# An RWKV-5 layer fused with a squared-ReLU FFN: the logarithm of w taken on a spread tile, two chunks' small matmuls interleaved, and another order in the opening

## The chip, the cores and the metric

The kernel runs on one core of one Trainium2 chip. The metric is the device time of one execution in microseconds (us), given as the median of the runs. Times inside the execution come from one profiled execution and are counted from the start of its span. The engines are named as in the profile: PE (TensorE; PEld is its weight load), DVE (VectorE), ACT (ScalarE), POOL (GpSimd) and SP (SyncE, which here only issues DMAs). Each engine works through its own instructions strictly in order and waits on semaphores for what the others produce.

## The reference

```
def _attn_ref(r, k, v, w, u):                      # (4, 8, 768, 48): batch, heads, sequence, head_dim
    state = zeros((B, H, D, D))
    for t in range(S):
        cur = einsum('bhd,bhe->bhde', u[None] * kt, vt)
        y[:, :, t] = einsum('bhd,bhde->bhe', rt, state + cur)
        state = w[None, :, :, None] * state + einsum('bhd,bhe->bhde', kt, vt)

def _moe_ref(x, w_in, w_out):                      # 3072 tokens, 384 -> 2048 -> 384
    h = maximum(x @ w_in, 0.0)
    return h * h @ w_out
```

A linear-attention recurrence with a decay `w` per head and channel is computed over 768 steps, its output is laid out as 3,072 rows of 384, and a dense layer pair with a squared ReLU between follows.

## The kernel before

The sequence is cut into chunks of 128 steps. A unit is one batch element and one chunk (24 units, list `UNITS`); within a chunk the recurrence is done in the parallel form, and a state `S0W` per batch element is handed from chunk to chunk. The decay enters as powers of w: `Wt` = exp(t·ln w) multiplies r (step `rh`), `Wk` = exp(-(t+1)·ln w) multiplies k (step `kh`). These factors come from ln w, which is laid out over all 128 partitions.

Each step of the program is a small function of class `Do`; the string `ORDER` lists all steps as `name.unit:engine/buffer` in the order in which they are put into the engines' queues. So the order on one engine is the order of that engine's entries in the string, and the place between entries of different engines has no force. The number behind the slash picks the buffer or the PSUM bank (eight banks).

The steps that matter here, for a unit i or a pair q of units:

- `w`, `u`: DMA of the two parameter rows, issued by ACT; `tab` loads ACT's table. `lw` (L266) takes Ln of the row w on one partition into `lrow`; `bw` (L269) spreads that over 128 partitions with a matmul by a row of ones into a PSUM bank; `Wt`, `Wk` (L298, L294) take Exp of that bank, scaled by a column of t. `bu`, `ub` (L272) spread u; `bc`, `WLcol`, `WLm` (L303, L309, L314) make the decay over a whole chunk.
- `lp.x.q` (L325): load of r, k or v for both units of a pair (384 KB in runs of 384 bytes), `ld.x.i` (L321): the same for a single unit (192 KB in runs of 192 bytes). SP issues both. `V.q` (L331) loads a quarter of the first FFN matrix into `W1[q]`, `W.q` (L334) a quarter of the second into `W2[q]`; GpSimd issues these, because the DMA casts to bf16 on its way.
- The first four units are done in two pairs (`PAIRED = 4`): pair 0 is both chunks 0 and 1 of batch 0, pair 1 those of batch 1. A pair's tile holds the even and the odd steps of 256 steps as two tiles of 128 partitions; partitions 0 to 63 belong to the first chunk, 64 to 127 to the second. `TR`, `TK` (L364) transpose r and k on PE, `RC`, `KC` copy the result out of PSUM (ACT, L251), `Ap` (L384) makes the scores, `Bp` (L392, DVE) masks them.
- `U.i` (L463) makes a chunk's contribution to the state, `S0` (L478) decays it into `S0W`. `Y.i` makes the output of a chunk: for a paired unit two matmuls with an identity that add `dv` (L428), four that add the old state (L436, second chunk only), and sixteen scores times v (L440).
- `P0`, `P1`, `du`, `dv` (L343, L347, L350, L355) make the bonus term with u; `vb` (L251 or L253) casts v to bf16.
- `xs` copies the output, `X` (L489) transposes it on PE, `xTc` copies that; then the FFN: `F1` (L505), `re` (relu), `sq` (square), `F2` (L533), `os`, `out`.
- `mP.0`, `mP.1`, `mJ` build the masks on GpSimd (L283, L220, L278). `Z.n` (L565) is n identity matmuls into a bank that nobody reads.

The memsets ahead of the string (L204 to L234) all run on DVE: the padding of `lrow`, the ones, the padding of the seven `rk` tiles, and `WLm`.

Of the kernel before, what the change touches and what calls it, by code (L numbers as in the profile page):

```python
# [19 lines left out]
EARLY_U = ()  # L20
COLS = (slice(0, 288), slice(288, 384))
GROUPS = [1, 1, 2, 2, 2, 2, 2, 2, 2, 2, 2, 2, 1, 1]
POOLS = dict(ldr=8, ldk=8, ldv=8, ws=3, rk=7, P=5, dv=5, vb=8, rkT=7, bank=8, Bm=8, xs=5, xT1=2, xT2=3, hr=6, hq=28,
    os=8, ts=2)
ORDER = """
w:A mP.0:G mP.1:G lp.r.0:S/0 lp.k.0:S/0 tab:A lw:A Z.8:P/0 bw:P/0 lp.r.1:S/1 lp.v.0:S/0 mJ:G u:A lp.k.1:S/1 Wt.1:A/1
lp.v.1:S/1 bc:P/2 P0.1:G/0 Wk.0:A/3 rh.1:D/0 ld.r.5:S/4 Wt.0:A/4 bu:P/5 kh.0:D/1 V.3:G WLcol:A P0.0:D/1 Wk.1:A/6
rh.0:D/1 TR.0:P/7 ld.k.4:S/4 V.0:G rh.3:D/2 ub:A V.1:G rh.2:D/3 vb.0:A/0 vb.1:A/1 ld.r.4:S/5 kh.1:D/0 P1.0:G RC.0:A/0
TR.1:P/2 kh.2:D/3 kh.3:D/2 TK.0:P/1 KC.0:A/1 V.2:G P1.1:D U.1:P/5 Z.2:P/4 TK.1:P/4 ld.k.5:S/5 du.0:D/0 dv.0:G RC.1:A/2
du.1:D/1 dv.1:G Ap.0.1:P/7/3 Bp.0.1.1:D/0 vb.3:A/2 U.0:P/6 Ap.0.0:P/1/2 Bp.0.1.0:D/1 Bp.0.0.1:D/2 WLm:G KC.1:A/3  # L30
Z.7:P/3 Ap.1.0:P/3/7 vb.2:A/3 U.3:P/2 Bp.0.0.0:D/3 P0.2:G/2 U.2:P/4 S0.0:D Y.0:P/1 ld.v.4:S/4 S0.2:D P1.2:G Y.1:P/6
xs.0:A/0 ts.3:D/0 ts.1:D/1 X.0:P/4 Ap.1.1:P/1/2 xTc.0:D/0 du.2:D/2 xs.1:A/1 X.1:P/5 F1.0.3:P/4 xTc.1:A/1 P0.3:G/3
P1.3:G Bp.1.0.1:D/4 F1.0.0:P/6 re.0.3:D/0 dv.2:G F1.1.3:P/5 Wt.2:A re.0.0:A/1 W.1:G Bp.1.1.1:D/5 du.3:D/3 ld.v.5:S/5
Bp.1.0.0:D/6 Wk.2:A F1.1.0:P/4 F1.1.1:P/6 dv.3:G re.1.0:A/2 F1.0.1:P/0 rh.5:G/4 re.1.3:A/3 Bp.1.1.0:D/7 Y.3:P/4
sq.1.3:A/0 re.0.1:A/4 W.2:G kh.4:D/5 re.1.1:A/5 sq.1.0:D/1 Y.2:P/5 ld.k.6:S/6 xs.3:D/2 W.3:G F1.0.2:P/0 xs.2:A/3
rh.4:D/5 sq.0.0:A/2 X.3:P/6 W.0:G X.2:P/4 re.0.2:D/3 F1.1.2:P/5 xTc.3:A/0 sq.0.3:A/3 xTc.2:D/0 re.1.2:A/2 P0.4:D/4
T.4:P/0 Tc.4:D/4 F1.2.4:P/6 F1.2.7:P/4 sq.1.2:D/4 F1.2.5:P/5 re.2.4:D/1 re.2.7:A/0 ld.r.6:S/6 sq.0.2:A/5 F1.2.1:P/0
re.2.5:D/2 re.2.1:A/3 sq.2.5:D/6 sq.0.1:D/7 F1.2.0:P/6 kh.5:D/4 F1.2.2:P/4 sq.2.1:A/8 F1.2.6:P/5 re.2.2:A/2 re.2.0:D/4
T.5:P/0 re.2.6:D/3 F2.0.2:P/4 F1.2.3:P/6 ld.r.7:S/7 Tc.5:A/5 P1.4:D du.4:D/4 sq.1.1:D/9 A.4:P/5/0 sq.2.6:A/10
re.2.3:A/5 sq.2.3:A/11 F2.0.1:P/4 sq.2.0:A/12 F2.0.3:P/4 vb.4:G/4 Bm.4.1:D/0 Bm.4.0:D/1 sq.2.7:A/13 P0.5:D/1 A.5:P/6/0  # L40
Bm.5.1:D/2 sq.2.4:A/14 F2.1.1:P/5 Bm.5.0:D/3 F2.1.2:P/5 ld.k.7:S/7 dv.4:G Y.4:P/0 P1.5:G du.5:D/0 F2.3.2:P/6
sq.2.2:A/15 ld.v.7:S/6 ld.k.9:S/0 xs.4:D/4 F2.0.0:P/4 vb.5:A/5 Y.5:P/0 dv.5:D xs.5:D/0 F2.3.0:P/6 P0.6:G/0 P1.6:G
ld.v.6:S/7 F2.3.1:P/6 os.0:D/0 ld.r.9:S/0 X.4:P/0 xTc.4:D/1 U.4:P/4 F2.1.0:P/5 X.5:P/0 F2.1.3:P/5 S0.4:D xTc.5:D/1
rh.7:G/6 F1.3.0:P/4 os.1:D/1 F1.3.4:P/0 P0.7:G/2 re.3.0:D/3 out.1:S F1.3.2:P/5 kh.7:D/6 re.3.4:A/5 kh.6:G/0 F1.3.6:P/4
re.3.6:A/4 ld.r.8:S/1 vb.6:A/6 re.3.2:A/0 XB.7:S/6 rh.6:D/0 F1.3.3:P/0 F2.3.3:P/6 kh.9:D/1 re.3.3:A/1 P1.7:D XB.6:S/1
F2.2.2:P/4 os.3:D/2 F1.3.1:P/5 du.7:D/1 S.1:D ld.k.8:S/1 U.5:P/0 S0.5:D dv.7:G U.6:P/6 re.3.1:A/2 sq.3.1:A/16
F2.2.3:P/4 ld.r.11:S/2 ts.6:D/1 F2.2.1:P/4 sq.3.3:D/17 P0.9:G/3 sq.3.0:A/18 ld.r.10:S/3 F2.2.0:P/4 sq.3.6:A/19
F1.3.7:P/0 os.2:D/3 du.6:D/2 A.7:P/5/6 ld.k.11:S/2 re.3.7:A/2 vb.7:G/7 F1.3.5:P/4 Bm.7.1:D/0 sq.3.2:A/20 rh.8:G/2
# [76 lines left out]
def kernel(  # L125
# [511 lines left out]
```

## Time and profile before

| | |
|---|---|
| median of 3 runs | 170.58 us (170.56 to 170.84) |
| the profiled execution's own time | 171.19 us |
| its span | 169.5 us |
| granted TensorE clock over the span | 1.00 |
| DMA, mean over the span | 163 GB/s |

How to read what follows: a row of the timeline gives the start in us from the span's start, the time from the first start to the last end of the instructions merged into it, engine, line of the kernel, operation, tile written, tiles read, shape, the count after an x, and in brackets the engine's idle time before it with what ended that. An end of a matmul is modelled, so the start of the next one is the better mark of when PE was free. The bracket of a DMA queue's row ("q1", "q0") gives packets, megabytes and the time that the packets took as a share of 16 DMA engines over the window; two packets can be in flight on one engine, so a share can exceed 100%. Queue q1 is SP's, q0 is GpSimd's.

### The profile page before, as it was taken

To read this page: it belongs to the slowest core of one execution; us is meant where nothing else is said; L and a number is where in the kernel's file an instruction comes from. 1 tells how busy PE (TensorE), PEld (TensorE's weight loads), DVE (VectorE), ACT (ScalarE), POOL (GpSimd) and SP (SyncE) were. 2 spreads that over 40 slices of the span, in tenths; PEclk is the share of its full clock that TensorE was granted. 3 is DMA by queue.
4 is the path that set the end of the run, shared out by engine and by line. 5 is a ranking of instruction groups with operands and counts; after the bars stand their busy time and mean duration, and the time that the engine had idled before them with its cause. 6 is when DMAs were issued, how large, how long until landed. Compare 5 with 4: busy or idle time off the path is not lost.

```text
span 169.5 us, 4602 instructions
## 1 busy us (share of the span) xinstructions
PE 164.2 (97%) x1828; PEld 125.4 (74%) x1828; DVE 137.1 (81%) x255; ACT 101.9 (60%) x190; POOL 99.9 (59%) x122
## 2 busy tenths in 40 slices
PE   4999999999999999999999999999999999999993
PEld 1686989767866786888766888766888676898762
DVE  5669989997899999979999999998779975955300
ACT  4684686870685779249892359952099393254731
POOL 6799681277199608996699979399627550200000
PEclk9999999999999999999999999999999999999999
DMA  5999999991899798999997999965959672230032
GB/s 136 323 237 193 215 215 208 201 200 39 165 200 211 138 191 173 209 201 134 209 203 151 212 228 220 177 136 141 184 98 202 170 88 70 90 99 0 6 139 93
DMA packets 96137, 27.56 MB, mean 163 GB/s; under 512 B 90642, under 2 KB 96020, under 8 KB 96116
## 3 DMA queue, kind: packets, MB, share of 16 engines
q1 hardware_dynamic: 92416, 22.55, 66.4%
q0 software_dynamic: 2816, 3.54, 11.5%
q10 hardware_dynamic: 884, 1.18, 2.2%
q8 instruction: 14, 0.23, 0.6%
q14 instruction: 7, 0.06, 0.1%
HBM read 20.45 MB, written 4.72 MB: 149 GB/s over the span
## 4 chain that ended last, share of the span: by engine, by line
PE 95%; ACT 1%; DVE 1%; issue 1%; ACTq 0%
PE bank L505 37%; PE bank L533 36%; PE bank L411 3%; PE bank L463 2%; PE bank L452 2%; PE bank L364 2%; PE bank L489 2%; PE bank L450 2%; PE bank L547 2%; PE bank L440 1%; PE bank L269 1%; DVE Bm L392 1%; PE bank L303 1%; PE bank L272 1%; PE bank L398 1%; PE bank L428 1%
## 5 line engine op out<-in xcount | busy, mean ns | idle before, releaser
L505 PE MATMUL bank<-xT,W 128*128 128x256 bf16 (+1 forms) x672 | 70.0, 257 | 0.0
L533 PE MATMUL bank<-W,hq 128*128 128x384 bf16 x368 | 68.9, 326 | 0.0
L505 PEld LDWEIGHTS <-W 128*128 128x128 bf16 x672 | 56.9, 98 | 7.7
L515 ACT ACTIVATE hr<-bank 128x512 bf16<-128x512 f32 x67 | 38.7, 594 | 36.4 <-PE bank L505 27.8
L533 PEld LDWEIGHTS <-hq 128*128 128x128 bf16 x368 | 33.8, 98 | 18.2
L522 ACT ACTIVATE hq<-hr 128x512 bf16<-128x512 bf16 x70 | 41.0, 626 | 3.4 <-DVE hr L517 2.8
L419 DVE TENSOR_TENSOR Bm<-bank,maskJT 128x512 bf16<-128x512 f32 x40 | 25.7, 682 | 2.7 <-PE bank L411 2.7
L355 POOL TENSOR_TENSOR dv<-ldv,du 128x384 f32<-128x384 f32 (+1 forms) x18 | 15.9, 891 | 16.2 <-DVE du L350 11.3
L517 DVE TENSOR_SCALAR hr<-bank 128x512 bf16<-128x512 f32 x29 | 19.7, 686 | 6.6 <-PE bank L505 4.5
L347 POOL TENSOR_TENSOR P<-P,ub 128x384 f32<-128x384 f32 x15 | 16.0, 1070 | 13.1 <-DVE P L343 12.7
L340 POOL TENSOR_TENSOR rk<-ldr,Wt 128x384 bf16<-128x384 f32 x15 | 16.4, 1101 | 0.0
L343 POOL TENSOR_TENSOR P<-ldr,ldk 128x384 f32<-128x384 f32 x13 | 13.3, 1023 | 1.5 <-DMA ldk<-in_k_dram 1.2
L524 DVE TENSOR_TENSOR hq<-hr 128x512 bf16<-128x512 bf16 x26 | 12.4, 490 | 2.0 <-ACT hr L515 1.8
L484 POOL TENSOR_TENSOR S0W<-ts,WLm 128x384 bf16<-128x384 f32 x10 | 10.9, 1091 | 4.4 <-DVE ts L481 3.6
L475 DVE TENSOR_TENSOR xs<-bank,dv 128x384 bf16<-128x384 f32 x20 | 11.1, 553 | 3.0 <-PE bank L452 1.1
L337 POOL TENSOR_TENSOR rk<-ldk,Wk 128x384 bf16<-128x384 f32 x12 | 12.3, 1032 | 1.4 <-DMA ldk<-in_k_dram 1.4
L350 DVE TENSOR_REDUCE du<-P 128x8 f32<-128x384 f32 x24 | 12.9, 542 | 0.0
L253 DVE COPY os<-bank 128x384 f32<-128x384 f32 x11 | 6.1, 551 | 6.9 <-PE bank L533 6.9
L481 DVE TENSOR_TENSOR ts<-bank,S0W 128x384 f32<-128x384 f32 x16 | 8.7, 550 | 1.2 <-POOL S0W L484 0.8
L452 PE MATMUL bank<-vb,Bm 128*128 128x48 bf16 x160 | 9.5, 183 | 0.0
L251 ACT COPY os<-bank 128x384 f32<-128x384 f32 (+2 forms) x14 | 6.3, 458 | 4.5 <-PE bank L533 2.5
L452 PEld LDWEIGHTS <-Bm 128*128 128x128 bf16 x160 | 8.2, 96 | 1.0
(79 smaller groups left out, 177.8 us busy)
## 6 DMA issues: line engine op xcount, KB each, us to landing
ldr<-in_r_dram SPq DMA_DIRECT2D x20, 192.0 KB, 4.0
ldk<-in_k_dram SPq DMA_DIRECT2D x20, 192.0 KB, 4.2
ldv<-in_v_dram SPq DMA_DIRECT2D x20, 192.0 KB, 3.6
out_dram<-os SPq DMA_DIRECT2D x12, 192.0 KB, 2.1
W<-in_moe_w_in_dram POOLq DMA_DIRECT2D x4, 384.0 KB, 8.6
W<-in_moe_w_out_dram POOLq DMA_DIRECT2D x4, 384.0 KB, 6.4
out_dram<-os ACTq DMA_DIRECT2D x5, 192.0 KB, 3.5
ldr<-in_r_dram SPq DMA_DIRECT2D x2, 384.0 KB, 4.1
```

What stands on the lines that cost most here:

```text
L340: e.tensor_mul(rk[slot[f"rk{i}"]][:, 0, :, 0:D], loaded("r", i), Do.factor("t", i % 2 if i < PAIRED else 2))
L343: e.tensor_mul(P0b[slot[f"P{i}"]], loaded("r", i), loaded("k", i))
L347: e.tensor_mul(t, t, bank("bu")[:, 0 : H * D].rearrange("p (h d) -> p h d", h=H) if i in EARLY_U else ub)
L350: e.tensor_reduce(dub[slot[f"dv{i}"]], P0b[slot[f"P{i}"]], axis=mybir.AxisListType.X, op=ALU.add)
L355: e.tensor_mul(dv_of(i) if i < PAIRED else dvb[slot[f"dv{i}"]], loaded("v", i), t)
L419: e.tensor_mul(Bmb[slot[f"Bm{i}{h}"]], heads(bank(f"bA{i}{h}"), 128), mask_b)
L452: e.matmul(y[:, hc, D * h : D * (h + 1)], m[h][:, hc, :], vb[:, 2 * hc + h, :], start=(c == 0), stop=True, skip_group_check=True,)
L505: e.matmul(hp[:, fi, :], W1[f // 4][:, c, 256 * (f // 2 % 2) : 256 * (f // 2 % 2 + 1)].rearrange("p (m j) -> p j m", j=2)[:, f % 2, :], xt ...
L515: e.activation(hr, hp, AF.Relu)
L517: e.tensor_scalar_max(hr, hp, 0.0)
L522: e.activation(hq, hr, AF.Square)
L533: e.matmul(bank(f"bO{i}")[:, 0:d_model], hqb[slot[f"hq{g},{f // m}"]][:, at : at + L], W2[q][:, f % 4, :], start=(seen[i] == 1 and f % 4 = ...
```

## The change

1. `bw` now spreads w itself, and `lw` takes Ln of the spread rows: from the PSUM bank (128 x 384) into an SBUF tile `LW`. `Wt` and `Wk` take Exp of `LW` in place of the bank; `bc` reads row 0 of `LW`.
2. `U` of both chunks of a pair becomes `UP.q`, `Y` of both becomes `YD.q` (dv and scores of both chunks) and `YI.i` (the state's part for the second chunk). In both, a matmul on partitions 0 to 63 and one on 64 to 127 alternate. The instructions are as many as before.
3. GpSimd's queue begins with `mP.1 mR mP.0 V.0 mW V.3 V.2 V.1` in place of `mP.0 mP.1 mJ P0.1 V.3 V.0 V.1 P1.0 V.2`. `mR` (padding of three `rk` tiles) and `mW` (`WLm`) were DVE memsets. `mJ` comes much later.
4. The opening has another order: SP loads `r.0 k.0 k.1 v.1 r.1 v.0` (before: `r.0 k.0 r.1 v.0 k.1 v.1`); `Z.8`, `Z.2` and `Z.7` are gone, one `Z.4` is new; each engine's own order is as below. From about the fortieth microsecond on, each engine has the same steps in the same order as before, with other banks.

```
PE   before: Z.8 bw bc bu TR.0 TR.1 TK.0 U.1 Z.2 TK.1 Ap.0.1 U.0 Ap.0.0 Z.7 Ap.1.0 U.3 U.2 Y.0 Y.1 X.0 Ap.1.1 X.1 F1...
PE   after:  bw bc bu TR.0 TK.0 TK.1 Z.4 Ap.0.1 Ap.0.0 TR.1 UP.1 UP.0 YD.0 Ap.1.1 YI.1 X.0 Ap.1.0 X.1 F1...
ACT  before: w tab lw u Wt.1 Wk.0 Wt.0 WLcol Wk.1 ub vb.0 vb.1 RC.0 KC.0 RC.1 vb.3 KC.1 vb.2 xs.0 xs.1 xTc.1
ACT  after:  w tab u lw Wt.1 Wt.0 Wk.1 Wk.0 ub RC.0 KC.0 KC.1 vb.0 WLcol vb.3 vb.2 vb.1 RC.1 xs.0 xs.1 xTc.1
DVE  before: rh.1 kh.0 P0.0 rh.0 rh.3 rh.2 kh.1 kh.2 kh.3 P1.1 du.0 du.1 Bp (pair 0, 4) S0.0 S0.2 ts.3 ts.1 xTc.0
DVE  after:  nj rh.1 rh.0 P0.0 kh.1 kh.0 P0.1 kh.2 kh.3 P1.0 du.0 du.1 rh.2 rh.3 Bp (pair 0, 4) S0.2 S0.0 du.2 Bp.1.1.0 xTc.0
POOL before: mP.0 mP.1 mJ P0.1 V.3 V.0 V.1 P1.0 V.2 dv.0 dv.1 WLm P0.2 P1.2 P0.3 P1.3 dv.2 W.1 dv.3 rh.5 W.2 W.3 W.0 vb.4
POOL after:  mP.1 mR mP.0 V.0 mW V.3 V.2 V.1 P1.1 P0.2 dv.1 dv.0 WLm P1.2 P0.3 dv.2 P1.3 dv.3 W.2 kh.4 mJ W.1 W.3 rh.5 W.0 vb.4
SP   before: lp.r.0 lp.k.0 lp.r.1 lp.v.0 lp.k.1 lp.v.1 ld.r.5 ld.k.4 ld.r.4 ld.k.5 ...
SP   after:  lp.r.0 lp.k.0 lp.k.1 lp.v.1 lp.r.1 lp.v.0 ld.k.4 ld.r.5 ld.r.4 ld.k.5 ...
```

```diff
-    nc.vector.memset(lrow[:, :, D:64], 0.0)
+    nc.vector.memset(LW[0:1, :, D:DP], 0.0)
     nc.vector.memset(ones, 1.0)
+    for t in rk[:PAIRED]:
+        nc.vector.memset(t[:, :, :, D:DP], 0.0)
...
-    for t in rk:
-        nc.vector.memset(t[:, :, :, D:DP], 0.0)
-    nc.vector.memset(WLm, 0.0)
...
-        def lw(e):
-            e.activation(lrow[:, :, 0:D], wrow.rearrange("a (h d) -> a h d", h=H), AF.Ln)
-        def bw(e):
-            e.matmul(bank("bW")[:, 0 : H * D], ones, lrow[:, :, 0:D], start=True, stop=True)
+        def bw(e):
+            e.matmul(bank("bW")[:, 0 : H * D], ones, wrow, start=True, stop=True, skip_group_check=True)
+        def lw(e):
+            e.activation(LW[:, :, 0:D], bank("bW")[:, 0 : H * D].rearrange("p (h d) -> p h d", h=H), AF.Ln)
+        def mR(e):
+            for t in rk[PAIRED:]:
+                e.memset(t[:, :, :, D:DP], 0.0)
+        def mW(e):
+            e.memset(WLm, 0.0)
...
+        def spreading(e, o, scale):
+            e.activation(o, LW[:, :, 0:D], AF.Exp, scale=scale)
...
+        def YD(e, q):
+            y = [heads(bank(f"bY{2 * q + x}"), 2 * D) for x in range(2)]
+            for a in range(2):
+                for x in range(2):
+                    e.matmul(y[x][Do.half(a)], identity[Do.half(x), Do.half(x)],
+                             dv_of(2 * q + a)[Do.half(x)]..., start=True, stop=False)
+            for hc in range(HP):
+                for h in range(2):
+                    for a in range(2):
+                        for x in range(2):
+                            e.matmul(y[x][:, hc, D * h : D * (h + 1)], Bmb[slot[f"Bm{q}{a}{h}"]][Do.half(x), hc, :],
+                                     vbb[slot[f"vb{2 * q + a}"]][Do.half(x), 2 * hc + h, :], start=False, stop=True)
+        def YI(e, i):
+            for hc in range(HP):
+                e.matmul(y[:, hc, :], rT[:, hc, i % 2, :], S0W[UNITS[i][0]][:, hc, :], start=False, stop=True)
...
+        def UP(e, q):
+            o = [heads(bank(f"bU{2 * q + x}"), 2 * D) for x in range(2)]
+            for hc in range(HP):
+                for a in range(2):
+                    for x in range(2):
+                        e.matmul(o[x][:, hc, :], pair(rk[slot[f"rk{2 * q + a}"]], 1, hc)[Do.half(x)],
+                                 vbb[slot[f"vb{2 * q + a}"]][Do.half(x), 2 * hc : 2 * hc + 2, :]..., start=(a == 0), stop=(a == 1))
```

More of the change, by code (lines that the diff above doesn't have):

```diff
@@ L19 @@
 PAIRED = 4
-EARLY_U = ()
 COLS = (slice(0, 288), slice(288, 384))
 GROUPS = [1, 1, 2, 2, 2, 2, 2, 2, 2, 2, 2, 2, 1, 1]
-POOLS = dict(ldr=8, ldk=8, ldv=8, ws=3, rk=7, P=5, dv=5, vb=8, rkT=7, bank=8, Bm=8, xs=5, xT1=2, xT2=3, hr=6, hq=28,
-    os=8, ts=2)
+POOLS = dict(ldr=8, ldk=8, ldv=8, rk=7, P=5, dv=5, vb=8, rkT=7, Bm=8, xs=5, xT1=2, xT2=3, hr=6, hq=28, os=8, ts=2, bank=8)
 ORDER = """
-w:A mP.0:G mP.1:G lp.r.0:S/0 lp.k.0:S/0 tab:A lw:A Z.8:P/0 bw:P/0 lp.r.1:S/1 lp.v.0:S/0 mJ:G u:A lp.k.1:S/1 Wt.1:A/1
@@ L27 @@
[L27 to L36, printed above, removed]
@@ new lines @@
+TR.0:P/5 Wk.1:A/6 P0.0:D/0 kh.1:D/1 Wk.0:A/7 kh.0:D/0 mP.1:G TK.0:P/0 ub:A P0.1:D/1 lp.v.1:S/1 kh.2:D/2 mR:G kh.3:D/3
+RC.0:A/0 KC.0:A/1 lp.r.1:S/1 TK.1:P/4 KC.1:A/2 lp.v.0:S/0 vb.0:A/0 Z.4:P/7 mP.0:G WLcol:A P1.0:D du.0:D/0 V.0:G mW:G
+V.3:G V.2:G V.1:G P1.1:G du.1:D/1 Ap.0.1:P/6/5 P0.2:G/2 rh.2:D/2 vb.3:A/1 dv.1:G vb.2:A/2 rh.3:D/3 vb.1:A/3 dv.0:G
+Bp.0.1.0:D/0 WLm:G P1.2:G Ap.0.0:P/0/7 Bp.0.1.1:D/1 TR.1:P/3 RC.1:A/3 Bp.0.0.0:D/2 UP.1:P/1/4 UP.0:P/2/6 Bp.0.0.1:D/3
+YD.0:P/5/0 Ap.1.1:P/7/3 S0.2:D S0.0:D YI.1:P P0.3:G/3 xs.0:A/0 X.0:P/1 du.2:D/2 xs.1:A/1 dv.2:G Bp.1.1.0:D/4
@@ L213 @@
     njcol = const.tile([128, 3], FP32, name="njcol")
-    nc.vector.tensor_scalar(njcol, tcol, -1.0, -1.0, op0=ALU.mult, op1=ALU.add)
     identity = const.tile([128, 128], BF16, name="identity")
@@ L260, in u, with bu, ub @@
             e.dma_start(out=urow, in_=u.rearrange("h d -> (h d)").rearrange("(a n) -> a n", a=1))
+        def bw(e):
+            e.matmul(bank("bW")[:, 0 : H * D], ones, wrow, start=True, stop=True, skip_group_check=True)
+        def bu(e):
+            e.matmul(bank("bu")[:, 0 : H * D], ones, urow, start=True, stop=True, skip_group_check=True)
+        def ub(e):
+            copy(e, ub.rearrange("p a b -> p (a b)"), bank("bu")[:, 0 : H * D])
         def tab(e):
@@ L265, in lw, with nj @@
         def lw(e):
-            e.activation(lrow[:, :, 0:D], wrow.rearrange("a (h d) -> a h d", h=H), AF.Ln)
-        def bw(e):
-            e.matmul(bank("bW")[:, 0 : H * D], ones, lrow[:, :, 0:D], start=True, stop=True)
-        def bu(e):
-            e.matmul(bank("bu")[:, 0 : H * D], ones, urow, start=True, stop=True)
-        def ub(e):
-            copy(e, ub.rearrange("p a b -> p (a b)"), bank("bu")[:, 0 : H * D])
+            e.activation(LW[:, :, 0:D], bank("bW")[:, 0 : H * D].rearrange("p (h d) -> p h d", h=H), AF.Ln)
+        def nj(e):
+            e.tensor_scalar(njcol, tcol, -1.0, -1.0, op0=ALU.mult, op1=ALU.add)
+        def mR(e):
[3 more added lines that the diff above has]
+            e.memset(WLm, 0.0)
         def mJ(e):
@@ L303, in bc @@
                 e.matmul(
-                    bank("bc")[:, hc : hc + 1], pair(lrow.rearrange("p (o a) b -> p o a b", o=1), 0, hc), ones[:, 0:1],
+                    bank("bc")[:, hc : hc + 1], pair(LW[0:1].rearrange("p (o a) b -> p o a b", o=1), 0, hc), ones[:, 0:1],
                     start=True, stop=True, skip_group_check=True,
@@ L346, in P1 @@
             t = P0b[slot[f"P{i}"]]
-            e.tensor_mul(t, t, bank("bu")[:, 0 : H * D].rearrange("p (h d) -> p h d", h=H) if i in EARLY_U else ub)
+            e.tensor_mul(t, t, ub)
         def du(e, i):
@@ L419, in Bm, with half @@
             e.tensor_mul(Bmb[slot[f"Bm{i}{h}"]], heads(bank(f"bA{i}{h}"), 128), mask_b)
+        def half(x):
+            return slice(64 * x, 64 * x + 64)
+        def YD(e, q):
+            y = [heads(bank(f"bY{2 * q + x}"), 2 * D) for x in range(2)]
+            for a in range(2):
+                for x in range(2):
+                    e.matmul(
+                        y[x][Do.half(a)], identity[Do.half(x), Do.half(x)],
+                        dv_of(2 * q + a)[Do.half(x)].rearrange("p (a e) d -> p a (e d)", e=2),
+                        start=True, stop=False, skip_group_check=True,
+                    )
+            for hc in range(HP):
+                for h in range(2):
+                    for a in range(2):
+                        for x in range(2):
+                            e.matmul(
+                                y[x][:, hc, D * h : D * (h + 1)],
+                                Bmb[slot[f"Bm{q}{a}{h}"]][Do.half(x), hc, :],
+                                vbb[slot[f"vb{2 * q + a}"]][Do.half(x), 2 * hc + h, :],
+                                start=False, stop=True, skip_group_check=True,
+                            )
+        def YI(e, i):
+            y = heads(bank(f"bY{i}"), 2 * D)
+            rT = rkTb[slot[f"rT{i // 2}"]].rearrange("p x y -> p (x y)").rearrange("p (h c t) -> p h c t", h=HP, c=2)
+            for hc in range(HP):
+                e.matmul(
+                    y[:, hc, :], rT[:, hc, i % 2, :], S0W[UNITS[i][0]][:, hc, :],
+                    start=False, stop=True, skip_group_check=True,
+                )
         def Y(e, i):
@@ L599 @@
         at = [int(a) if a.isdigit() else a for a in at]
-        held = [h.format(*at) for h in HELD.get(name, [])]
+        x = 2 * at[0] if at and isinstance(at[0], int) else 0
+        held = [h.format(*at, x=x, y=x + 1) for h in HELD.get(name, [])]
         if name in ("xTc", "xX"):
```

211 lines of the change are left out of this document (97 added, 114 removed).

## The prediction

> **What bounds the kernel now.** I read the page first, then the opening engine by engine in the timeline, then the DMA queues in windows.
>
> ```profile
> span 169.5 us, 4602 instructions
> PE 164.2 (97%) x1828; PEld 125.4 (74%) x1828; DVE 137.1 (81%) x255; ACT 101.9 (60%) x190; POOL 99.9 (59%) x122
> PE 95%; ACT 1%; DVE 1%; issue 1%; ACTq 0%
> ```
>
> PE fills the span and the chain. In the windows it is full from the first FFN matmul on:
>
> ```profile
> 18.13:20.00 1.87, 1.87 (x37) 1.87 (x35) 1.87 (x4) 1.30 (x3) 1.46 (x2) 1.00 1.22 208
> 30.00:40.00 10.00, 10.00 (x102) 6.70 (x101) 8.96 (x18) 6.20 (x11) 5.85 (x6) 1.00 0.92 178
> ```
>
> So the kernel is an opening until the first `F1`, and then a PE stream of fixed work. A change in the opening is worth the shift of the first `F1`, plus the PE work saved behind it. This is PE's opening:
>
> ```profile
> 3.24 1.64 PE L269 MATMUL bank<-lrow,ones 1*128 1x384 f32 x2 [0.24 <-ACT lrow L266]
> 6.25 1.62 PE L272 MATMUL bank<-urow,ones 1*128 1x384 f32 x2
> 7.80 2.74 PE L364 MATMUL bank<-identity,rk 128*128 128x128 bf16 x24
> 12.38 0.42 PE L384 MATMUL bank<-rkT,rkT 48*64 48x128 bf16 x16
> 14.79 0.70 PE L463 MATMUL bank<-vb,rk 64*128 64x96 bf16 x16 [0.19 <-DVE Bm L392]
> 15.42 0.35 PE L428 MATMUL bank<-dv,identity 64*64 64x384 bf16 x2
> 16.49 0.34 PE L436 MATMUL bank<-S0W,rkT 128*128 128x96 bf16 x4
> 17.27 0.34 PE L489 MATMUL bank<-identity,xs 128*128 128x128 bf16 x3
> 18.13 4.18 PE L505 MATMUL bank<-xT,W 128*128 128x128 bf16 x72
> 22.24 0.35 PE L428 MATMUL bank<-dv,identity 64*64 64x384 bf16 x2
> 24.09 0.84 PE L505 MATMUL bank<-xT,W 128*128 128x128 bf16 x12
> ```
>
> The first `F1` is at 18.13. The second pair's `Y.3`, `Y.2` take PE from 22.24 to 24.09, 1.85 us.
>
> **The change, part by part: the W1 quarters.** This decides my forecast. GpSimd's rows:
>
> ```profile
> 1.86 0.22 POOL L283 MEMSET maskP<- 128x128 bf16 x1
> 2.84 0.20 POOL L283 MEMSET maskP<- 128x128 bf16 x1
> 3.80 0.20 POOL L278 MEMSET maskJT<- 128x128 bf16 x1
> 5.61 0.99 POOL L343 TENSOR_TENSOR P<-ldr,ldk 128x384 f32<-128x384 f32 x1 [1.24 <-DMA ldk<-in_k_dram]
> 6.55 2.50 POOL L331 DMA_DIRECT2D W<-in_moe_w_in_dram  x3
> ```
>
> Before, the first quarter stands behind `P0.1`, which waits for a load of k: it is issued at 6.55. After, only `mP.1`, `mR` and `mP.0` stand ahead, and none of them waits for data. A mask takes 0.97 us (1.86 to 2.84); `mR` is three memsets, put at 0.22 us each by the mask's. So `V.0` is issued at 1.86 + 0.97 + 0.66 + 0.97 = 4.5 us. The pad's shape has no row on GpSimd; even 0.5 us a memset makes it 5.3. What the queues then do is seen in windows of 2.5 to 9.5, 9.5 to 10.5 and 11 to 18 us, in this order:
>
> ```profile
> q1 hardware_dynamic: 5876, 2.23, 115.2%
> ...
> q0 software_dynamic: 147, 0.15, 91.8%
> q1 hardware_dynamic: 237, 0.08, 31.3%
> ...
> q0 software_dynamic: 1123, 1.10, 92.7%
> q1 hardware_dynamic: 1212, 0.23, 27.9%
> ```
>
> Alone, SP's queue moves 5876 / 7 = 839 packets a us. With W1 beside it, it moves 1212 / 7 = 173 and W1 160: packet for packet, and W1's are 1 KB against 192 bytes. The small loads fall to a fifth of their pace. Before, this hits nobody: the first W1 packet comes after 9.5, about 3.0 us behind its issue, when the pair loads are nearly through.
>
> The pair loads are 6 x 1024 = 6,144 packets (384 KB in runs of 384 bytes), W1 is 4 x 384 = 1,536. After, W1's first packet comes at 4.5 + 3.0 = 7.5. By then 839 x 5.0 + some 130 (those before 2.5) = 4,330 load packets are done. W1 needs 1,536 / 160 = 9.6 us, to 17.1; beside it go 1,536 x 1.08 = 1,660 loads. The last 150 take 0.2 us, landing some 0.2 more: `lp.v.0`, now the last of the six, lands at **17.5 us**. If W1 starts sooner this hardly moves, because the same packets are to go; it falls only if W1 starts later: 13.6 for a start at 8.7, 10.6 (its time if nothing hits it) from 9.5 on. Before, v of pair 0 had landed 4.8 to 5.1 us behind its issue at 3.10, so by 8.3, where `vb.0` reads it; below it, what the steps of the chain take:
>
> ```profile
> 3.10 1.15 SPq L325 DMA_DIRECT2D ldv<-in_v_dram  x1
> ...
> DMA to landing us min/median/max: 4.8/5.0/5.1
> ...
> 8.29 0.93 ACT L251 CAST vb<-ldv 128x384 bf16<-128x384 f32 x2
> 10.62 1.93 ACT L251 COPY rkT<-bank 128x1024 bf16<-128x1024 bf16 x2 [0.50 <-ACT rkT L251]
> 11.18 1.61 POOL L355 TENSOR_TENSOR dv<-ldv,du 128x384 bf16<-128x384 f32 x2 [0.37 <-DVE du L350]
> 12.75 0.74 POOL L314 COPY WLm<-wcol 48x192 f32<-48x192 f32 x2
> 12.85 2.49 DVE L392 TENSOR_TENSOR Bm<-bank,maskP 128x512 bf16<-128x512 f32 x4 [1.30 <-PE bank L384]
> 15.25 1.01 DVE L478 TENSOR_TENSOR S0W<-bank,WLm 128x384 bf16<-128x384 f32 x2
> 17.64 0.36 DVE L253 COPY xT<-bank 128x384 bf16<-128x384 bf16 x1 [0.33 <-PE bank L489]
> ```
>
> What stands behind the late load: ACT's queue holds `vb.0`, then `WLcol vb.3 vb.2 vb.1 RC.1 xs.0`; GpSimd holds `dv.1 dv.0 WLm`. From 17.5: four casts at 0.47 and `WLcol` 0.1 end at 19.5; `UP.0` (16 matmuls, 0.4 to 0.63) ends at 20.1; `YD.0` (1.2, below) at 21.3; `Ap.1.1` 0.4, `YI.1` 0.3: 22.0. GpSimd's side is level with that: dv 1.6, `WLm` 0.75 end at 19.9, two `S0` at 20.9, ahead of `YI.1`. `RC.1` (1.0) ends at 20.5. From the end of `Y.1` (17.27) to `F1` it took 0.86 before; so the first `F1` is at 22.0 + 0.86 = **22.9**, against 18.13: +4.7. r of pair 1 lands between 12 and 16 us and delays `rh.2`, the masks `Bp` (2.5) and `TR.1`, to 19.6 at most, under the same wait.
>
> **PE's clock.** PE then waits, but for eight transposes, from about 11.6 to 19. In the trace it starts slow: 24 transposes at 7.80 take 114 ns each, while 72 `F1` of the same width take 58. That it falls back after a wait no row shows; the bounds are 0 and, if it is slow again from 19.1 for the 4.6 us that it was before (7.80 to 12.38), half of that, 2.3. Much of these 4.6 us is ACT's and DVE's work, so I take 0.9.
>
> The Trainium skill has a rule here ("TensorE: Matmul & The Clock Gate", Part 1): an idle window of about 3.4 us puts PE at half clock, and some 3.4 us of activity take it back. The row of slow transposes agrees with the second half; no row of before shows the first. By that rule the sum would carry up to 1.7 us here, without it 0.
>
> **The other parts.**
>
> ```profile
> 1.97 1.03 PE L565 MATMUL bank<-identity 128*128 128x512 bf16 x2 [1.97 <-DVE njcol L214]
> ...
> 2.67 0.52 ACT L266 ACTIVATE lrow<-wrow 1x384 f32<-1x384 f32 x1
> 4.92 0.56 ACT L298 ACTIVATE bank<-bank,tcol 128x384 f32<-128x384 f32 x1 [1.73 <-PE bank L269]
> ```
>
> `Ln` takes 0.56 after `bw` instead of 0.52 before it (an ACT pass over 128 x 384 is 0.56 in L298's rows), so the chain to `Wt` is as long; `bw` may start when w has landed, at most 1.1 us sooner than 3.24 (`Z.8` ends at 3.0). PE still has `bc` and `bu` ahead of the transposes, so 0.2 us of it arrives there. All this, `ts` leaving DVE's path, the warm-up matmuls and the better order (`KC.0` right behind `RC.0`) lie under the wait for v and gain nothing; without that wait they are the rival below. `mR` and `mW` leave DVE, where they lay before any data.
>
> Interleaving: sixteen `Ap` matmuls alternating over array parts start every 25 ns (0.42 us for 16), sixteen `U` every 39 (14.79 to 15.42). `YD.1` and `YI.3` replace 1.85 us: 32 scores at 25 to 31 ns are 0.8 to 1.0, dv and state 0.3 each: 1.4, a saving of 0.45, behind the first `F1` and so real. Bounds: 0.65 saved, or 0.5 lost if the alternation itself costs (the change from dv to scores leaves a hole of 0.25 each time). What `UP` and `YD.0` save in front is in the chain above.
>
> **Sum** against the profiled execution: 171.19 + 4.7 + 0.9 - 0.45 = 176.3. That execution was 0.61 over the median of 170.58; so **175.7 us**. W2 is issued 5 us later as well, but its consumers shift alike.
>
> **The rivals.**
> (a) *The squeeze does not come*, since W1's first packet is still after 9.5 (GpSimd's start or the first packet is slower than I take them). For it: the 3.0 us rest on a single first issue. Against: every row ahead of `V.0` is short. Then `lp.v.0` lands at 10.6; `TR.0` starts at 7.6, behind bc and bu; `RC.0`, `KC.0` end at 9.5 and 10.5, `Ap` starts at 10.6 (12.38 before); DVE, with `P1.0`, `du`, `rh.2`, `rh.3` ahead, begins the four `Bp` at 11.4 and ends at 13.9; `YD.0` is at 14.1 (`Y.0` 15.42), and the first `F1` at 16.8: 171.19 - 1.3 - 0.45 - 0.61 = **168.8**. Faster: the other sign. From a start of W1 at about 8.8 on the change is no loss, from 9.5 on it has all of this.
> (b) *Half a squeeze*: W1's first packet at 8.7. By then 5,330 load packets are done, the other 810 take 4.7 us at 173; v lands at 13.6, the first `F1` comes 5.4 us behind it at 19.0: 170.58 + 0.9 - 0.45 = **171.0**, and up to 173.7 for a start at 8.
> (c) *The full clock loss*: 2.3 in place of 0.9, and interleaving saves nothing: **177.6**. I count it as the upper end of the forecast.
>
> The Trainium skill ("DMA: Bandwidth & Descriptors", Queues, rings and completion order) says that each DMA engine takes turns between its queues packet by packet, which speaks for the squeeze whatever the size of the loads' packets; the equal counts from 11 to 18 us agree. Its first-byte figure for GpSimd's path, about 1 us, would start W1 at 5.5 and leave (a) and (b) little room; the 3.0 us here are longer.
>
> **How the numbers follow.** Forecast with (c): 0.72, from 173.5 to 177.8. (b): 0.12. (a): 0.16. Of (b), 0.02 fall within 0.2% of before (what a measurement of this kernel tells from no change is about 0.2%) and of (a) 0.01. Faster 0.15, same 0.03, slower 0.82. The range for 8 in 10 takes in the forecast's own and most of (b): 170.2 to 177.8.
>
> **What would show it.** In the timeline of after: `V.0` issued at 4.3 to 5.3; q0's packets from 6.5 to 7.7 on, level with q1's and far below 839 a us for q1; `vb.0` with a long wait for ldv until about 17.5; a hole on PE up to 19; the first `F1` at 22 to 24; transposes or `F1` at over 100 ns there if the clock fell. `YD.1` to the next `F1` in 1.4 us. Wrong if `vb.0` starts by 12: then (a). If v is late and yet `F1` comes before 20, the chain behind it is mis-sized. If the first `F1` is at 22.9 and the time is below 173.5, PE's stream has slack I did not see.

## The result, and the profile after

| | before | after |
|---|---|---|
| median | 170.57 us (170.53 to 170.84, 4 runs) | 178.88 us (177.94 to 179.63, 4 runs) |
| the profiled execution's own time | 171.19 us | 179.63 us |
| its span | 169.5 us | 177.9 us |
| granted TensorE clock over the span | 1.00 | 0.96 |
| start of the first `F1` | 18.13 us | 25.89 us |

The changed kernel is slower by a factor of 1.048 (interval 1.045 to 1.051). It is slower in the way that was forecast, and by 3.2 us more than forecast. On the chips of the later experiments some executions, of the kernel before (about 175 us) and of four others, took some 2 to 3% longer than the rest; the medians and ratios below leave these out.

The page of after: its span, the granted clock in forty slices of 4.4 us, and the chain's shares by engine.

```profile
span 177.9 us, 4595 instructions
...
PEclk9997557999999999999999999999999999999999
...
PE 87%; DMA 8%; SPq 2%; ACT 1%; issue 0%; ACTq 0%
```

PE's share of the chain went from 95% to 87%, a DMA took 8% (14 us), and in the slices from 13 to 31 us the clock falls to half. Both are new. The timeline of GpSimd shows what starts it:

```profile
4.43 0.94 POOL L338 DMA_DIRECT2D W<-in_moe_w_in_dram  x1
...
19.75 1.61 POOL L362 TENSOR_TENSOR dv<-ldv,du 128x384 bf16<-128x384 f32 x2 [5.12 <-DMA ldv<-in_v_dram]
```

`V.0` goes out at 4.43, 2.1 us before the first quarter of the kernel before; `dv` in the second row, which needs v, begins only at 19.75. The first packet of W1 moves at 6.96, by the start of the packets in the trace. The queues in the windows from 7 to 11 us (first two rows) and from 11 to 18 us:

```profile
q0 software_dynamic: 476, 0.47, 71.1%
q1 hardware_dynamic: 1093, 0.41, 44.8%
...
q0 software_dynamic: 1049, 1.04, 87.4%
q1 hardware_dynamic: 1072, 0.40, 32.6%
```

From 11 to 18 us the two queues move 150 and 153 packets a us: turn for turn, the loads at 153 where they had 839 alone. Here is the chain of waits through that stretch (start, length, what), then ACT's row:

```profile
5.43 14.18 DMA ldv<-in_v_dram
...
19.64 0.03 ACT vb L247
```

```profile
19.64 0.51 ACT L247 CAST vb<-ldv 128x384 bf16<-128x384 f32 x1 [8.02 <-DMA ldv<-in_v_dram]
```

`lp.v.0` takes 14.18 us from its issue, against 4.8 to 5.1 before; ACT sits 8.02 us idle for it, GpSimd 5.12. PE's timeline after that, and its clock in windows (window, length, busy time and count of PE, PEld, DVE, ACT and POOL, then granted clock, DMA share, GB/s):

```profile
14.12 0.86 PE L371 MATMUL bank<-identity,rk 128*128 128x128 bf16 x8 [2.25 <-DVE rk L347]
21.09 1.47 PE L478 MATMUL bank<-vb,rk 64*128 64x96 bf16 x32 [6.10 <-ACT vb L247]
...
25.89 4.45 PE L529 MATMUL bank<-xT,W 128*128 128x128 bf16 x48
30.28 0.36 PE L435 MATMUL bank<-dv,identity 64*64 64x384 bf16 x4
30.57 0.57 PE L444 MATMUL bank<-vb,Bm 64*128 64x48 bf16 x32
31.07 0.34 PE L455 MATMUL bank<-S0W,rkT 128*128 128x96 bf16 x4
31.25 0.83 PE L529 MATMUL bank<-xT,W 128*128 128x128 bf16 x12
```

```profile
15.00:16.00 1.00, 0.00 (x0) 0.01 (x1) 1.00 (x3) 0.00 (x0) 0.00 (x0) 0.80 1.19 205
16.00:17.00 1.00, 0.00 (x0) 0.00 (x0) 0.92 (x2) 0.00 (x0) 0.00 (x0) 0.50 1.20 207
...
28.00:29.00 1.00, 1.00 (x13) 1.00 (x11) 0.00 (x0) 0.52 (x2) 0.98 (x3) 0.50 1.21 245
29.00:30.00 1.00, 1.00 (x18) 1.00 (x17) 0.00 (x0) 0.00 (x0) 0.93 (x2) 0.87 1.06 209
```

PE works 0.86 us between 12 and 21 us. By the granted clock's column it falls to half in the sixteenth microsecond and stays there until past 29, so the chain behind v and most of the first 48 `F1` run at half rate: 4.45 / 48 = 93 ns for an `F1` in the mean (the first 32 start 107 ns apart, the rest 56), against 4.18 / 72 = 58 before. Last, the interleaved `YD.1` and `YI.3`, already at full clock, take from 30.28 to 31.25: 0.97 us in place of 1.85.

The account, from rows of both kernels: the first `F1` is 25.89 - 18.13 = 7.8 us later; 48 `F1` at half clock cost about 4.45 - 48 x 0.058 = 1.7 more; the interleaving gives back 0.9. That is 8.6, and the spans differ by 8.4.

### The profile page after: what moved, and what is told of

It reads as the page before. It is cut to its first block, busy times and chain, and to the rows that moved or that the text cites. A ratio compares the mean times of both kernels' runs of the same rounds, so it can differ in the third digit from the quotient of the medians.

```text
span 177.9 us, 4595 instructions
## 1 busy us (share of the span) xinstructions
PE 163.8 (92%) x1821; PEld 125.7 (71%) x1821; DVE 135.7 (76%) x252; ACT 101.4 (57%) x189; POOL 100.3 (56%) x126
## 4 chain that ended last, share of the span: by engine, by line
PE 87%; DMA 8%; SPq 2%; ACT 1%; issue 0%; ACTq 0%
PE bank L529 36%; PE bank L557 34%; DMA ldv<-in_v_dram 8%; PE bank L418 3%; SPq L332 2%; PE bank L468 2%; PE bank L513 2%; PE bank L466 2%; PE bank L488 2%; PE bank L571 1%; PE bank L478 1%; PE bank L405 1%; PE bank L444 1%; PE bank L391 1%; ACT vb L247 0%
## 5 line engine op out<-in xcount | busy, mean ns | idle before, releaser
L529 PE MATMUL bank<-xT,W 128*128 128x256 bf16 (+1 forms) x672 | 71.8, 262 | 0.0
L529 PEld LDWEIGHTS <-W 128*128 128x128 bf16 x672 | 58.5, 100 | 7.6
L350 POOL TENSOR_TENSOR P<-ldr,ldk 128x384 f32<-128x384 f32 x12 | 12.4, 1037 | 4.2 <-DMA ldr<-in_r_dram 4.2
L344 POOL TENSOR_TENSOR rk<-ldk,Wk 128x384 bf16<-128x384 f32 x13 | 13.3, 1027 | 1.0 <-DMA ldk<-in_k_dram 0.9
L247 ACT CAST vb<-ldv 128x384 bf16<-128x384 f32 x12 | 5.8, 507 | 10.3 <-DMA ldv<-in_v_dram 8.0
```

The source lines that it names most:

```text
L344: e.tensor_mul(rk[slot[f"rk{i}"]][:, 1, :, 0:D], loaded("k", i), Do.factor("k", i % 2 if i < PAIRED else 2))
L529: e.matmul(hp[:, fi, :], W1[f // 4][:, c, 256 * (f // 2 % 2) : 256 * (f // 2 % 2 + 1)].rearrange("p (m j) -> p j m", j=2)[:, f % 2, :], xt ...
```

## The experiments

**When W1 is issued, and nothing else.** Two kernels are the changed one with one or two more builds of a mask, which nobody needs, ahead of `V.0` on GpSimd. They delay W1's issue by 0.96 us each and change nothing in the queues of the other engines.

```diff
 du.0:D/0
+mP.1:G
 V.0:G
```

One build more:

> The changed kernel with one more building of mask mP.1 (the same values) on GpSimd ahead of V.0, nothing else moved: V.0 is issued 0.97 us later, at 5.4. Theory (packets taken in turns from W1's first packet on): the first packet comes at about 8.0 in place of 7.0, 4,750 of the 6,144 load packets are done, the rest goes at 150 a us: lp.v.0 lands at 17.0 to 18.5 in place of 19.6, the first F1 comes at 23 to 24.7, 176 to 178 us. Rival (what counts is only that W1 is issued before the last loads, not when): 178.4 to 179.6 as the changed kernel.

Two builds more:

> The same with two more buildings of the mask: V.0 is issued at 6.4, where the kernel with P0.1 ahead of it has it, but P0.1 stays on DVE and every other engine's queue is the changed kernel's. Theory: the first packet at about 9.0, v of pair 0 lands between 10.5 and 13.5, the first F1 at 17.3 to 19.2, no clock of 0.5 after the first F1, 169.8 to 171.8 us. Rival (moving P0.1 off DVE brought the gain, not W1's later issue): 177 us or more.

Timeline of the kernel with one build more (GpSimd, ACT, PE):

```profile
5.39 0.94 POOL L338 DMA_DIRECT2D W<-in_moe_w_in_dram  x1
...
16.25 0.51 ACT L247 CAST vb<-ldv 128x384 bf16<-128x384 f32 x1 [4.61 <-DMA ldv<-in_v_dram]
...
22.50 4.48 PE L529 MATMUL bank<-xT,W 128*128 128x128 bf16 x48
```

And of the kernel with two:

```profile
6.35 0.94 POOL L338 DMA_DIRECT2D W<-in_moe_w_in_dram  x1
...
11.67 0.54 ACT L247 CAST vb<-ldv 128x384 bf16<-128x384 f32 x1
...
17.30 3.14 PE L529 MATMUL bank<-xT,W 128*128 128x128 bf16 x48
```

| extra builds | `V.0` issued | first W1 packet | `lp.v.0` landed | first `F1` | clock | median, us | ratio to before |
|---|---|---|---|---|---|---|---|
| 0 (after) | 4.43 | 6.96 | 19.62 | 25.89 | 0.96 | 178.88 | 1.048 (1.045 to 1.051) |
| 1 | 5.39 | 8.29 | 16.23 | 22.50 | 0.97 | 174.69 | 1.025 (1.021 to 1.029) |
| 2 | 6.35 | 9.67 | 10.34 | 17.30 | 1.00 | 170.31 | 0.996 (0.995 to 0.997) |

Less than 2 us of GpSimd's time decide 8.6 us of the kernel's. With two builds the cast's row has no wait for ldv at all. The whole loss is W1's start; what else the change does is worth 0.4% in its favour. With one build the landing came 0.8 us, the time 1.3 us below the low end of what was expected.

**The gate of before, put back.** The same aim with a useful step in place of idle builds: `P0.1` goes from DVE back to GpSimd, ahead of `V.0`, where its wait for k holds W1 up.

```diff
-P0.1:D/1
 ...
 du.0:D/0
+P0.1:G/1
 V.0:G
```

> The changed kernel with one step moved: P0.1, which waits for the load of k of pair 0, goes from DVE to GpSimd, ahead of the first W1 quarter. Theory (W1's packets squeeze the last pair loads, v of pair 0 comes late, PE idles and loses its clock): V.0 is issued at about 6.6 us in place of 4.4, its first packet comes at about 9.2, lp.v.0 lands between 11 and 12.5 in place of 19.6, the first F1 is at 16.8 to 17.8, the granted clock does not fall to 0.5 there, and the time is 168.5 to 170.0 us, below both kernels. Rival (the order of the opening, the banks, the missing warm-up matmuls or the interleaving itself cost the 8 us): the time stays above 174.

Its timeline:

```profile
6.56 0.94 POOL L338 DMA_DIRECT2D W<-in_moe_w_in_dram  x1
...
17.43 3.10 PE L529 MATMUL bank<-xT,W 128*128 128x128 bf16 x48
```

Median 170.36 us, 0.999 of before (0.995 to 1.002), clock 1.00. The loss is gone, but no gain is left: the time is level with the kernel before and misses the 168.5 to 170.0 that were expected. In the profiled execution, the fastest of them (169.86), the first `F1` comes 0.7 us before that of the kernel before; rival (a) had that at 16.8 and so took the gain of the new order for too large.

**The early issue alone, in the kernel before.** Its four quarters go out right behind `mP.1`:

```diff
 mP.1:G
+V.3:G V.0:G V.1:G V.2:G
 lp.r.0:S/0
```

> The kernel before with nothing but the four W1 quarters moved up in GpSimd's queue, behind the two pair masks and ahead of P0.1. Theory: W1's first packet at about 6.5 us, the last two pair loads (here k and v of pair 1) land at about 13 and 19 us instead of 9.1 and 10.6, vb.3 on ACT holds up what stands behind it, first F1 at 23 to 26, a clock of 0.5 in between, 175 to 180 us. Rival (order, banks or warm-up are the cause, not W1's place): within 1 us of 170.6.

Its timeline on GpSimd and PE, and the page's clock:

```profile
3.69 3.27 POOL L332 DMA_DIRECT2D W<-in_moe_w_in_dram  x4
...
17.65 1.07 PE L365 MATMUL bank<-identity,rk 128*128 128x128 bf16 x8 [6.17 <-DVE rk L338]
...
27.19 6.27 PE L506 MATMUL bank<-xT,W 128*128 128x128 bf16 x72
```

```profile
PEclk9996555999999999999999999999999999999999
```

Median 181.72 us, 1.063 of before (1.059 to 1.067): 1.7 us above the range that was expected, and worse than the whole change. W1's first packet moved at 7.16, `lp.v.1` landed at 19.31, within 0.4 us of the late load in after. Here k and v of pair 1 come last, and the order of PE puts pair 1's transposes ahead of pair 0's scores, so PE is held from 11.5 on. The early issue does it in either kernel. Of the 2.6 us by which this span (180.5) is above that of after, the interleaving alone is worth 1.3 (below).

**The clock.** Two kernels are the changed one with idle identity matmuls (`Z`), which keep PE at work while it waits for v, so that only the clock differs. `Z.n` stands for n blocks of 128 columns, four of them to a matmul, so `Z.112` is 28 matmuls of 512 columns. In the first kernel these stand ahead of `UP.1`:

```diff
 Bp.0.0.0:D/2
+Z.112:P/4
 UP.1:P/1/4
```

> The changed kernel with 28 identity matmuls of 512 columns put on PE ahead of UP.1, in the hole in which PE waits for v; they end before v comes and nothing reads them. It prices the clock alone. Theory: v lands at 19.6 as before, the clock stays at 1.00 or returns to it before 21, the first F1 comes at 25.0 to 25.5 in place of 25.9 and the first F1 matmuls start every 58 ns and not every 93: 176.0 to 177.0 us against 178.9. Rival (the fall of the clock lies under waits of ACT and DVE): 178.5 to 179.3.

PE in its timeline:

```profile
16.11 8.06 PE L589 MATMUL bank<-identity 128*128 128x512 bf16 x28
24.11 0.85 PE L478 MATMUL bank<-vb,rk 64*128 64x96 bf16 x32
...
27.15 2.84 PE L529 MATMUL bank<-xT,W 128*128 128x128 bf16 x48
```

The 28 take 288 ns each in the mean, where those of the next kernel take 222: the first eight start 427 ns apart, those from the tenth on 216, so the first ones still ran at half speed, and the fill ended 3 us too late, `UP.1` starting at 24.11 in place of 21.09. Yet the median is 179.56 us (178.64 to 179.71) and the span 178.0, that of after. Behind the fill the matmuls run at the full pace (48 `F1` in 2.84 us), which gave back all of the 3 us; but as a price this run is spoilt, and it misses the 176.0 to 177.0 that were expected. The second try splits the fill, five ahead of `TR.1` and 25 ahead of `UP.1`:

```diff
+Z.20:P/4
 TR.1:P/3
 ...
+Z.100:P/4
 UP.1:P/1/4
```

> The changed kernel with identity matmuls on PE that nothing reads, sized to the holes: 5 of 512 columns ahead of TR.1 and 25 ahead of UP.1. The run with 28 behind TR.1 began cold and ended 3 us too late, at 24.1. Theory (the clock's fall costs PE time on the path): PE is back at full rate when v lands at about 19.6, UP.1 starts at 21.0 to 21.3 as in the changed kernel, the first F1 comes at 24.6 to 25.3 in place of 25.9, and YD.1 follows it by 2.8 to 3.1 us in place of 4.4: span 175.0 to 176.0 against 177.9, time 176.3 to 177.5 us. Rival (the slow matmuls lie under ACT's and DVE's waits): UP.1 to YD.1 still takes 8.5 us or more, 178.5 us or more.

ACT and PE in its timeline:

```profile
19.70 0.51 ACT L247 CAST vb<-ldv 128x384 bf16<-128x384 f32 x1 [8.07 <-DMA ldv<-in_v_dram]
...
21.14 0.89 PE L478 MATMUL bank<-vb,rk 64*128 64x96 bf16 x32 [0.47 <-ACT vb L247]
...
24.69 2.84 PE L529 MATMUL bank<-xT,W 128*128 128x128 bf16 x48
```

```profile
PEclk9999999999999999999999999999999999999999
```

v is as late as in after (19.70 and 19.64) and `UP.1` starts at the same time, but the page's clock, the last line, is full throughout. The first `F1` is 1.2 us earlier and 48 of them take 1.6 us less: 2.8 us at that place, 2.2 of which reach the span (175.7 us). The medians differ by less, 177.33 against 178.88. So half clock costs 1.6 us here by the medians and 2.2 by the profiled executions; the rest is the late v, 7.0 us from 170.31, the kernel with two builds, to 177.33.

The price of the clock differs from one execution to the next. In the traces' records of the clock a stretch at half lasts a whole number of steps of 3.41 us: four in after (13.65 us), three with one build more (10.24), five in the early issue alone (17.07). Of the four executions of after two have a mean clock of 0.962 and took 179.35 and 179.63 us (the latter is the profiled one); two have 0.971 and took 177.94 and 178.42. One step fewer would give that 0.971 (an estimate: 1 - 0.5 x 10.24 / 176.2). The first two lie 2.2 us above the median of the filled kernel, the other two 0.85.

**The interleaving alone**, in the kernel before: `UP`, `YD`, `YI` in the places of `U` and `Y`, all else as it was.

```diff
-U.3:P/2 ... U.2:P/4 ... Y.3:P/4 ... Y.2:P/5
+UP.1:P/4/2 ... YD.1:P/5/4 YI.3:P
```

> The kernel before with the interleaving alone: UP.q in the place of U, YD.q and YI.i in the place of Y, W1 and the opening as they were. Theory: Y of pair 1 takes 1.0 us of PE instead of 1.85 as in the changed kernel's trace, and in the opening UP and YD save up to 0.4, of which the wait of YD.0 for S0.0 (a bank) may take as much: 169.3 to 169.9 us. Rival (alternating the halves of the array gains nothing, what the changed trace shows comes from elsewhere): 170.4 to 170.9.

PE in its timeline:

```profile
17.61 4.18 PE L549 MATMUL bank<-xT,W 128*128 128x128 bf16 x72
21.72 0.36 PE L464 MATMUL bank<-dv,identity 64*64 64x384 bf16 x4
22.01 0.57 PE L473 MATMUL bank<-vb,Bm 64*128 64x48 bf16 x32
22.52 0.34 PE L484 MATMUL bank<-S0W,rkT 128*128 128x96 bf16 x4
22.78 0.83 PE L549 MATMUL bank<-xT,W 128*128 128x128 bf16 x12
```

Median 169.62 us, 0.993 of before (0.991 to 0.996). `YD.1` and `YI.3` take 1.06 us in place of 1.85, and the first `F1` comes 0.52 sooner. Together 1.3, and the span is 168.2 against 169.5. This is the lowest median of all kernels run, below before and after; the kernels further down at 169.75 and 169.91, which hold the interleaving too, cannot be told from it.

**Ln on the spread rows alone**, in the kernel before (`LW` in place of `lrow`, `bw` ahead of `lw`, `Z.8` gone):

> The kernel before with the Ln part alone: w is spread first, Ln works on the spread tile, Wt, Wk and bc read it, and the eight warm-up matmuls ahead of bw are gone. My theory: the part lies under other work, so the first F1 moves by less than 0.3 us from 18.13, V.3 stays at about 6.5 us (P0.1 sets it) and the time is within 0.4 us of the kernel before (170.2 to 170.9). Rival: the Ln of 128 x 384 on the chain to Wt, or the missing warm-up, is part of the loss: Wt.1 starts after 5.3 us (4.92 before), the transposes start after 8.2 (7.80 before), and the time is above 171.2.

Median 170.73 us, 0.999 of before (0.997 to 1.001). `Wt.1` starts at 4.53 (4.92 before), the transposes at 7.84 (7.80), the first `F1` at 17.86. The part is hidden, as the forecast had it, and the warm-up matmuls of `Z.8` were not needed.

**Interleaving and Ln together**, that is the change without its order:

> The kernel before with the interleaved small matmuls and the Ln part, W1 still behind P0.1: the change without its order. My theory: the interleaving's gain stands (1.0 to 1.1 us for YD.1 and YI.3 in place of 1.85) and Ln adds or takes at most 0.3 us: 169.3 to 170.0 us, faster than the kernel before. Rival: the two parts disturb each other (the buffers' banks, the late Wt) and the gain is lost: 170.4 us or more.

Median 169.75 us, 0.995 of before (0.991 to 1.000): the gain of the interleaving, and none to be seen from Ln. The interval just reaches no change because of one execution of 171.96 us; the other five took 169.66 to 169.92. That one is the profiled one, and it shows on a small scale what the change does on a large one. The chain, then ACT and PE, then the clock's windows:

```profile
5.44 8.10 DMA ldv<-in_v_dram
```

```profile
13.55 0.51 ACT L251 CAST vb<-ldv 128x384 bf16<-128x384 f32 x1 [0.99 <-DMA ldv<-in_v_dram]
...
15.03 0.42 PE L382 MATMUL bank<-rkT,rkT 48*64 48x128 bf16 x16 [1.51 <-ACT rkT L251]
...
18.61 5.22 PE L547 MATMUL bank<-xT,W 128*128 128x128 bf16 x72
```

```profile
13.57:15.03 1.46, 0.00 (x1) 0.00 (x1) 1.46 (x3) 1.46 (x3) 1.30 (x3) 1.00 1.21 190
...
17.40:20.70 3.30, 3.30 (x42) 2.93 (x43) 2.31 (x5) 1.24 (x3) 1.96 (x3) 0.50 1.19 204
```

Fifteen of the sixteen DMA engines had delivered their part of `lp.v.1` by 10.6; the sixteenth, which presumably still had packets of it when W1 came, only at 13.53. PE waits 1.5 us, and from 2.3 us after that wait it has half clock for 3.4. So the gate of the kernel before, W1's first packet at about 9.5 with the pair loads through at 10.3 to 10.6, leaves little margin.

**A shorter path to the first `F1`.** The kernel with the gate, and `du.1` behind `rh.2` and `rh.3` on DVE, since the masks wait for these:

```diff
-du.1:D/1
 ...
 rh.3:D/2
+du.1:D/1
```

> The kernel with P0.1 on GpSimd ahead of V.0, and du.1 moved behind rh.2 and rh.3 on DVE, where it no longer waits 0.54 us for P1.1 with r of pair 1 already there. Theory: the four pair-0 masks begin at about 12.1 in place of 12.65, the first F1 at 16.9 to 17.2 in place of 17.43, the span 167.6 to 168.0 in place of 168.2. Rival (YD.0 waits for dv.0 or S0 for WLm on GpSimd just as long): the first F1 stays at 17.3 to 17.5.

PE in its timeline:

```profile
17.12 3.13 PE L529 MATMUL bank<-xT,W 128*128 128x128 bf16 x48
...
32.77 2.11 PE L557 MATMUL bank<-W,hq 128*128 128x384 bf16 x12 [0.19 <-DVE hr L541]
```

Median 169.91 us, 0.994 of before (0.993 to 0.996). The first `F1` is 0.31 earlier than with the gate alone, as expected, but the span, expected at 167.6 to 168.0, is the same, 168.2 us: at 32 us PE waits for DVE's relu, which it does not with the gate alone, and of the 0.31 there are 0.12 left at the scores behind it (34.72 against 34.84).

## Why the prediction was right in its mechanism and too small

The sign, the squeeze by W1 and the wait that it causes came as forecast, but the time of 178.88 us lies 3.2 us above the forecast and above the range, which ends at 177.8. Two terms of the sum failed by their size: the landing of `lp.v.0` and the clock.

- **W1's start**: right. `V.0` at 4.43 (4.5 predicted), the first packet 2.5 us behind (3.0), turn for turn with the loads from 11 us on.
- **The landing of `lp.v.0`, 17.5**: the first term that was mis-sized; it measured 19.62. The prediction let W1 go at 160 packets a us, which was its rate beside loads of 192-byte packets. Beside the pair's 384-byte packets it was 476 / 4 = 119 from 7 to 11 us and 150 after. And it took the mean engine for the last: the sixteen finished their parts of `lp.v.0` between 17.86 and 19.62, half of them by 18.7. So about 1.2 us are the rate and 0.9 the slowest engine. The step that the landing hardly depends on the start once W1 is early held: 19.62 for a start at 6.96, 19.31 for the last load with a start at 7.16 in the kernel before.
- **The chain from v to the first `F1`, 5.4**: right. At full clock it is 24.69 - 19.70 = 5.0; the 6.25 of after hold 1.2 of the clock's.
- **The clock, 0.9**: the second mis-sized term; it measured 2.2 us of the span, close to the upper bound of 2.3. That it fits the two executions of after with the shorter stretch at half (0.85) is luck. The prediction let PE be slow for 4.6 us after the wait, as at the start; it was slow from 21.09 to past 29, over 8 us, and the last 3.4 of these are `F1`s, which lose half of it. The Trainium skill ("TensorE: Matmul & The Clock Gate", Part 1) says that an idle window of some 3.4 us halves the clock, and that was in the text, but was kept out of the sum. The trace of after has the fall, with PE at work 0.86 us out of nine, though no 3.4 idle us stand ahead of it: before 15.60, where it comes, PE paused 2.25 us, made the eight transposes and paused 0.6 us. With the rule's 1.7 us in the sum the clock's term would have been nearer.
- **The way back to full clock**: the rule of the Trainium skill that the prediction quotes has some 3.4 us of activity for it, and the prediction sees this in the slow transposes of the kernel before. No trace here shows that: before, PE is at work from 3.24 on and its first record of full clock is at 12.29; after, it is at work again from 21.09 and has full clock from 29.25, 8.2 us later (with one build more 17.70 and 25.93, again 8.2). The first `F1`s, at 25.89 and 22.50, stand 3.4 us ahead of the return in both. Whether the small matmuls before them count for less was not tested.
- **The interleaving, 0.45**: half of what it was, 0.88 in after and 0.79 in the kernel before. The pace of alternating `Ap` matmuls, 25 ns, was taken for the scores; they took 0.50 / 32 = 16. Nor is 25 the pace of the `Ap`: by their starts in the trace four go off 3 to 4 ns apart, and 45 to 70 ns pass to the next four.
- **Ln, the warm-up, the moved memsets, at nothing**: right; Ln alone is 0.999 of before, and the change with W1 held up by two idle builds, 0.996, is no faster than the interleaving alone.
- **Rival (b)** needed only a later start. With one build more W1 began at 8.29, and by the prediction's sum, with the 153 packets a us that after measured for the loads, (6,144 - 4,990) / 153 = 7.5 us put the landing at 15.8; it measured 16.2.
- **Rival (a)** is what the two builds or the gate make of the change. It gave 168.8 and measured 170.3.

The sum goes over as follows: 17.5 to 19.6 adds 2.1, the chain takes off 0.4, the clock adds 1.3, the interleaving takes off 0.4. That is 2.6 of the 3.3 us by which the profiled execution (179.63) stands above the 176.3 worked out for it. With the 2.8 us that the clock cost at the first `F1`s themselves it is 3.2; why 0.6 of these did not come back in the span of the filled kernel was not traced.

What stayed open: why W1's pace was 119 packets a us in its first four microseconds. The packets show where it was lost: W1 moved 341 from 7 to 9.5 us, but 79 from 9.5 to 10.5, where the loads moved 467. The first quarter is 384 packets, and the second was issued 1.35 us behind it, so W1's queue may have run short there; no run tests it.

## What to carry to other kernels

A large transfer issued early on a second queue does not fill gaps: it takes every second turn, and small packets on the other queue fall to its pace, here from 839 to 153 a us. Before a load is moved up, count the packets still to go on the other queues at the time its first one lands, and time what waits for the last of them on the slowest DMA engine. A step that waits for data ahead of an issue may be the gate that keeps two queues apart; if it is taken away, another delay has to stand in its place.

## What the runs showed of the hardware that was not expected

- The scores of `YD`, 64 rows and 48 columns each, alternate over the two halves of the input's partitions and write two PSUM banks. 32 of them take 0.50 us, 16 ns each, in after and in the kernel with the interleaving alone. By their starts in the trace the two of a pair go off 3 to 4 ns apart, and the next pair 25 ns behind the last. The Trainium skill ("TensorE: Matmul & The Clock Gate", Part 1) says that the distance never falls below about 25 ns; these starts differ within a pair, and the measurement decides. Its Part 3 fits them better: matmuls on different tiles of the array run at the same time.
- Half clock can come without a pause of 3.4 us: in the profiled execution of interleaving and Ln together, the longest pause of PE once it was at work, 1.5 us, was followed, 2.3 us after its end, by 3.4 us at half clock. The rule of that page, no idle gap over 3.4 us, would not have warned of it. That the pause caused it is not shown; the five other executions of this kernel were not traced, read a clock of 1.00 and took 2 us less.
- The granted clock reads 1.00 from 8 to 10 us, as the row below, from a view of after, shows, although the 24 transposes that began at 7.71 took until 10.24, 105 ns each. The trace's records of the clock begin only at 12.19 us, and where there is no record the column reads 1.00. The trace of the first filled kernel has no such record at all, so its mean of 1.00 says nothing of its slow matmuls.

```profile
8.00:10.00 2.00, 2.00 (x21) 2.00 (x20) 1.97 (x4) 1.51 (x3) 1.11 (x2) 1.00 1.10 197
```
